# Rearranging the start, the masked KV product and the last tile of a gated SSM and linear-attention kernel under a new instruction order

## The chip, the cores and the metric

The kernel runs on one core of one Trainium2 chip. The metric is device microseconds of one execution. Executions of the same kernel on one core differ by one or two per cent here (163.33 to 166.11 us in 22 executions of the kernel before), so times are medians. An execution counts as slow when it is more than 1.5% above the fastest of its kernel in the same group; the medians below still include slow ones, the ratios do not. The traced execution has a span of its own, about 1.9 us shorter than its time (162.5 us for a time of 164.33 us before); places in the trace are given in microseconds from the start of that span.

## The reference, cut to what matters

The input is x, 2048 positions of 512 features. Two branches are mixed by a gate for each position.

```python
dt = exp(log_dt); Lam_bar = exp(dt * Lam)              # 512 complex poles
for t in range(L):                                      # branch A: a linear recurrence
    h = Lam_bar * h + B_bar @ x[t]
y = 2 * real(hseq @ Cmat.T) + x * Dskip
q, k, v = split(x @ wqkv)                               # branch B: 32 heads of 16
phi_q = concat(softmax(q @ w_phi), softmax(-q @ w_phi)) # 32 features a head
phi_k = concat(softmax(k @ w_phi), softmax(-k @ w_phi))
kv = phi_k.T @ v;  z = sum(phi_k)                       # over all positions
o = (phi_q @ kv) / (phi_q @ z + 1e-6)
g = sigmoid(sum(x * gate_w))
return g * y + (1 - g) * (o @ wo)
```

`kv` needs every position before the first output tile can use it. So there is a seam in the kernel.

## The kernel before

The kernel is a list of tasks, each with an engine, and a tuple `ORDER`, found by a search with assumed costs, that fixes in which order they are emitted; the traces show each engine taking its tasks in that order (VectorE's evacuation of x, whose transposes ended at 4.78 us, started at 6.07, behind the setup copies). Positions are taken in four phases of four tiles of 128.

The setup copies stand ahead of the plan on VectorE:

```python
for h in range(2):
    nc.vector.tensor_copy(out=sel[:, h, h:128:2], in_=ident[0:64, 0:64])
    nc.vector.tensor_copy(out=swap[:, h*64:h*64+64], in_=ident[:, 64-h*64:128-h*64])
# ... mask4, mask16, SM
```

x is transposed on TensorE, evacuated by ScalarE or VectorE, and used by V:

```python
t = pl.add(_pe(4, 128), tr, deps=[d_x[...]], bufs=[b, early[a // 2]])          # 4 transposes
xt[a, f] = evac_task(xT[:, :, tcols(f, a)], b, ..., [t], ("ACT", "DVE"), ...)
# ...
t = pl.add(_pe(4, 512), mm, deps=[xt[a, f], d_wv], bufs=[b])                   # V: 4 matmuls
```

At the seam, the accumulated KV of eight heads is masked to a block diagonal on VectorE, in four instructions, each followed by a small one for the sums `z` (SM). One element is 2 bytes; `(d h)` with h innermost means that the loop below, with d innermost, writes single values 16 bytes apart:

```python
VT(out=KVbd[qr, sgn].rearrange("p g (d h) -> p g h d", d=Dh)[:, :, half*4:half*4+4, :],
   in0=a4[:, :, :, 0:Dh],
   in1=mask4[pr].unsqueeze(1).unsqueeze(3).to_broadcast([64, HG, 4, Dh]), op=ALU.mult)
VT(out=SM[qr, sgn, :, 1, half*4:half*4+4], in0=a4[:, :, :, Dh], in1=..., op=ALU.mult)
```

After it TensorE does small matmuls (`SM`) for the denominators; ScalarE and VectorE make scale factors from them by logarithms and exponentials. For each output tile TensorE makes the numerators (`KVbd`), ScalarE and VectorE scale and add them, a DMA transposes the sum, and TensorE adds its product with Wo to the tile's branch-A matmuls in one PSUM bank. The bank is evacuated with the gate; the last tile's bank in two halves.

Of the kernel before, what the change touches and what calls it, by code (L numbers as in the profile page):

```python
# [18 lines left out]
P = 128  # L19
# [103 lines left out]
def kernel(  # L123
# [47 lines left out]
NWARM = 6  # L171
ORDER = (
    0, 6, 2, 4, 9, 176, 10, 14, 172, 13, 16, 168, 174, 184, 178, 156, 186, 180, 18, 182, 188, 20, 24, 191, 200,
    171, 192, 196, 202, 158, 195, 22, 164, 26, 228, 167, 232, 30, 220, 204, 230, 28, 248, 316, 32, 199, 222, 160,
    34, 132, 788, 36, 206, 78, 134, 234, 244, 138, 163, 236, 318, 154, 38, 794, 49, 792, 250, 136, 224, 240, 208,
    55, 238, 70, 140, 72, 67, 142, 660, 74, 227, 210, 144, 540, 420, 57, 246, 544, 46, 81, 77, 68, 82, 85, 148,
    790, 662, 547, 542, 146, 93, 424, 548, 44, 550, 59, 51, 422, 426, 242, 336, 328, 331, 324, 338, 554, 327, 332,
    796, 150, 42, 664, 334, 152, 667, 556, 558, 372, 346, 340, 376, 350, 514, 553, 96, 798, 53, 40, 668, 374, 348,
    344, 508, 670, 342, 352, 86, 516, 510, 560, 512, 518, 354, 378, 60, 356, 566, 673, 416, 358, 380, 382, 520,
    578, 562, 522, 418, 568, 800, 94, 524, 360, 384, 526, 386, 564, 362, 572, 388, 570, 364, 674, 390, 64, 602,  # L180
    580, 366, 394, 530, 574, 368, 532, 676, 396, 576, 680, 534, 370, 582, 686, 408, 62, 434, 678, 398, 606, 436,
    604, 688, 682, 692, 584, 596, 438, 98, 100, 528, 586, 684, 410, 476, 91, 698, 588, 690, 102, 104, 598, 482,
    108, 694, 400, 402, 700, 428, 106, 600, 590, 446, 696, 486, 702, 404, 112, 480, 448, 608, 484, 478, 610, 612,
    110, 704, 252, 430, 488, 212, 256, 450, 116, 114, 432, 440, 592, 412, 214, 706, 614, 392, 628, 254, 490, 442,
    258, 120, 216, 618, 492, 266, 118, 268, 494, 414, 620, 218, 498, 500, 458, 444, 452, 270, 454, 708, 460, 502,
    622, 88, 710, 504, 260, 124, 122, 616, 506, 536, 496, 538, 634, 406, 456, 712, 262, 630, 722, 278, 462, 716,
    638, 632, 636, 128, 714, 624, 464, 272, 264, 748, 274, 718, 126, 724, 720, 280, 466, 626, 754, 810, 276, 130,
    468, 726, 752, 750, 640, 642, 758, 644, 282, 290, 756, 728, 308, 646, 650, 284, 730, 470, 292, 812, 652, 594,
    732, 760, 734, 816, 762, 814, 648, 764, 286, 654, 738, 804, 320, 294, 820, 288, 808, 740, 472, 766, 656, 296,
    770, 742, 658, 312, 310, 822, 322, 864, 828, 314, 840, 298, 772, 774, 744, 746, 826, 776, 300, 778, 474, 818,  # L190
    834, 866, 782, 824, 786, 806, 868, 832, 784, 780, 870, 846, 842, 302, 882, 880, 876, 844, 836, 830, 878, 838,
    304, 848, 858, 914, 850, 852, 976, 884, 974, 1224, 888, 306, 978, 890, 980, 1230, 862, 892, 854, 894, 916,
    896, 886, 860, 874, 898, 856, 900, 1236, 982, 1072, 872, 908, 984, 1054, 986, 1074, 1056, 1024, 768, 1026,
    1096, 1100, 1102, 910, 988, 1076, 990, 1048, 1078, 920, 1050, 1080, 1218, 1058, 1052, 1030, 1098, 992, 1060,
    1082, 1032, 1226, 1228, 1000, 1062, 1006, 1066, 1222, 922, 994, 996, 1034, 1002, 1028, 1064, 1106, 1036, 1042,
    1234, 1104, 1086, 912, 1084, 902, 1008, 1010, 1232, 1038, 904, 998, 1088, 1238, 1220, 1004, 1108, 1014, 1012,
    918, 906, 1128, 932, 1068, 1040, 1240, 1152, 1110, 1154, 1044, 1146, 1016, 1090, 1070, 1148, 1018, 1200, 1122,
    934, 1248, 1156, 1112, 1130, 1092, 1046, 1132, 1114, 924, 1150, 1246, 1124, 1116, 1118, 1158, 944, 1176, 1244,
    1126, 1242, 1178, 1020, 1094, 1250, 1202, 1194, 1180, 1120, 1184, 1254, 1134, 1170, 1164, 1172, 1022, 1186,
    1160, 926, 1174, 1196, 1136, 1268, 1162, 1208, 936, 1204, 1140, 1252, 1274, 1182, 1256, 1270, 1188, 1138, 938,  # L200
    1346, 1198, 1258, 1166, 1206, 1260, 1340, 928, 940, 736, 1292, 1276, 1278, 942, 1168, 1212, 1298, 1348, 1262,
    1294, 1190, 1142, 1210, 930, 1342, 1214, 802, 1192, 1316, 1272, 1330, 1350, 956, 1344, 1352, 946, 948, 1306,
    1300, 1302, 1280, 1264, 968, 1318, 1322, 1296, 1216, 1266, 1354, 1324, 1356, 1332, 1320, 1326, 1328, 1308,
    950, 1144, 970, 1358, 1286, 1360, 1334, 958, 1304, 952, 1418, 1394, 1362, 1420, 1462, 1388, 1282, 962, 954,
    1396, 1284, 960, 1442, 1310, 1288, 1444, 1412, 1390, 1336, 1446, 1370, 1414, 1416, 1436, 1338, 1450, 1422,
    972, 1290, 1464, 964, 1364, 1372, 1424, 1438, 1366, 1426, 1312, 1378, 1314, 966, 1466, 1374, 1368, 1398, 1430,
    1376, 1392, 1452, 1402, 1428, 1400, 1382, 1432, 1404, 1380, 1440, 1448, 1434, 1406, 1408, 1384, 1454, 1456,
    1411, 1460, 1386, 1458)
# [5 lines left out]
def _pe(n, cols):  # L214
    return {"PE": n * max(30.0, cols / 2.4 + 3.0)}
# [11 lines left out]
def _fast_path(ctx, tc, A_x, A_Lambda_re, A_Lambda_im, A_B_re, A_B_im, A_C_re, A_C_im, A_log_dt, A_Dskip,  # L227
# [101 lines left out]
    nc.gpsimd.iota(iot[:], pattern=[[1, NCH]], base=0, channel_multiplier=0, allow_small_or_imprecise_dtypes=True)  # L329
    nc.gpsimd.memset(dgX[:], 0.0)  # L330
    nc.gpsimd.memset(KVbd[:], 0.0)
    nc.gpsimd.memset(SM[:], 0.0)
    nc.vector.memset(eps_t[:], 1e-6)
    nc.vector.memset(hpi_t[:], float(np.pi / 2.0))
    nc.vector.memset(vx[:, :, :, Dh:Dh + 1], 1.0)
    nc.vector.memset(Zs[:, :, :, 0:ZP], 0.0)
    nc.vector.memset(sel[:], 0.0)
    nc.vector.memset(sg[0:64, :], 1.0)
    nc.vector.memset(sg[64:128, :], -1.0)
    for h in range(2):  # L340
        nc.vector.tensor_copy(out=sel[:, h, h:128:2], in_=ident[0:64, 0:64])
        nc.vector.tensor_copy(out=swap[:, h * 64:h * 64 + 64], in_=ident[:, 64 - h * 64:128 - h * 64])
    nc.vector.tensor_reduce(out=mask4[:], in_=identf[:].rearrange("p (k m) -> p m k", m=4), axis=AX.X, op=ALU.add)
    nc.vector.tensor_reduce(out=mask16[:], in_=identf[:].rearrange("p (g e) -> p g e", e=16), axis=AX.X, op=ALU.add)
    for half in range(2):
        hp = slice(half * 64, half * 64 + 64)
        nc.vector.tensor_copy(out=SM[hp, :, :, 0, half * 4:half * 4 + 4],
                              in_=mask4[hp, :].unsqueeze(1).unsqueeze(1).to_broadcast([64, 2, HG, 4]))

    pl = _Plan({"DVE": 3.8e3, "ACT": 4.2e3, "PE": 1.0e3, "SP": 32.0e3})  # L350
# [40 lines left out]

    bw = pl.buf(*A1)
# [6 lines left out]
    xt = {}  # L399

    def x_block(a):
        pl.unit("x_block")
        for f in range(F):
            b = pl.buf(*A1)

            def tr(e, b=b, f=f):
                for kt in range(KT):
                    nc.tensor.transpose(bfv(b)[:, kt * P:(kt + 1) * P], xn[a][:, f, kt * P:(kt + 1) * P], ident[:])
            t = pl.add(_pe(4, 128), tr, deps=[d_x[a + (a > 0 or f > 1)]], bufs=[b, early[a // 2]])
            xt[a, f] = evac_task(xT[:, :, tcols(f, a)], b, lambda b: bfv(b).rearrange("p (k c) -> p k c", k=KT), [t],  # L410
                                 ("ACT", "DVE"), bf=True, rank=9)

    vt = {}

    def v_unit(ti):
# [7 lines left out]
        t = pl.add(_pe(4, 512), mm, deps=[xt[a, f], d_wv], bufs=[b])  # L423
# [34 lines left out]
    tpv = pl.add({"PE": 200.0}, p_vt, deps=[d_vec], bufs=[bv], rank=10)  # L458
# [26 lines left out]
    tp2 = pl.add({"DVE": 1400.0}, p2, deps=[tp1], rank=10)  # L485
# [35 lines left out]
    tp6 = pl.add({"DVE": 2000.0}, p6, deps=[tp3], rank=4)  # L521
# [10 lines left out]
    tp5 = pl.add({"DVE": 1500.0}, p5, deps=[tp4], rank=-2)  # L532
# [14 lines left out]
    for jj in range(2):  # L547
        parts = []
        for tt in range(4 * jj, 4 * jj + 4):
            parts.append(pl.add({"ACT": 210.0, "DVE": 165.0}, scaled(dgL[:, tt, :], ident[:], lr_[:, ucol(tt)]), deps=[tp3], rank=6 - jj))  # L550
            parts.append(pl.add({"ACT": 210.0, "DVE": 165.0}, scaled(dgS[:, tt, :], swap[:], ns1[:, ucol(tt)]), deps=[tp4], rank=6 - jj))
        t_dl.append(pl.add(_dve(256), lambda e, s_=slice(4 * jj, 4 * jj + 4): VT(out=dgL[:, s_], in0=dgL[:, s_], in1=dgS[:, s_], op=ALU.add),
                           deps=parts, rank=6 - jj))
        for h in range(2):
# [7 lines left out]
            t_dx.append(pl.add({"ACT": 320.0, "DVE": 340.0}, dx, deps=t_dl[-1:], rank=5 - jj))  # L562
    t_dd = [pl.add({"ACT": 210.0, "DVE": 165.0}, scaled(Dd[:, kt, :], ident[:], dsk[:, kt:kt + 1]), deps=[tv], rank=-5) for kt in range(KT)]
# [9 lines left out]
    for j in range(PT):  # L573
        done = []
        for ri in range(2):
            done.append(pl.add(_act(512), lambda e, j=j, ri=ri: nc.scalar.mul(out=tC[:, ri, :], in_=cb.t[:, 1 - ri, j, :], mul=nb2i[:, j:j + 1]),
                               deps=[tp6, t_cl] + tc_b[-2:], bufs=[cb], rank=2))
        for ri, c0 in enumerate((b2r, nb2r)):
# [3 lines left out]
            tc_b.append(pl.add(_dve(512), csc, deps=done, bufs=[cb], rank=2))  # L582
# [1077 lines left out]
```

## Time and profile before

| | before |
|---|---|
| time, median of 3 | 165.34 us (164.89 to 165.54) |
| span of the traced execution | 162.5 us |
| TensorE's wait ahead of V's first matmul, for the x evacuation that stands behind the setup copies | 1.8 us |
| TensorE's wait ahead of the small matmuls, for the KV product | 2.9 us |
| first matmul of the BT group | 23.34 us |
| VectorE's last sum of an output tile ends | 149.86 us |
| TensorE's last matmul to the end of the span | 5.6 us |

The waits come from the list of who waited for whom, the places from the timeline. The views themselves, the busy rows, the stretches, the chain that ended last and the seam, stand in the prediction with their reading.

### The profile page before, as it was taken

The numbers are of one execution on the slowest core, as the hardware profiler recorded it, in microseconds if no ns is written. First come the engines' busy times: TensorE is split into PE (matmuls) and PEld (weight loads), VectorE is DVE, ScalarE is ACT, GpSimd is POOL, SyncE is SP. The second block draws the span as 40 slices with busy tenths as digits, with TensorE's granted clock in tenths as the row PEclk, the third lists the DMA queues.
The fourth block names the chain that finished last, engine by engine and source line by source line (L and its number), as shares of the span: only waits on it lengthen the run. The fifth ranks groups of instructions, "written<-read, shape, count | busy, mean of one in ns | idle before, by whom it ended". The sixth has DMA issues, their size and how long they took to land.

```text
span 162.5 us, 3213 instructions
## 1 busy us (share of the span) xinstructions
PE 149.0 (92%) x1144; PEld 85.4 (53%) x1164; DVE 136.6 (84%) x370; ACT 113.6 (70%) x232; POOL 4.4 (3%) x12
## 2 busy tenths in 40 slices
PE   7599899999999999999999579999999999999960
PEld 2257466655564665655455145755755555554520
DVE  3517999898999899999999997999999999988030
ACT  3158799899878997878989728985892653492120
POOL 8200000000000000000000000000000000000000
PEclk9999999999999999999999969999999999999996
DMA  4989999200000222013522003013323224212531
GB/s 144 343 244 201 164 202 206 61 2 0 0 0 4 65 65 62 5 58 116 121 97 69 0 16 104 13 34 70 99 69 92 68 65 124 70 53 48 115 114 48
DMA packets 29998, 13.93 MB, mean 86 GB/s; under 512 B 23064, under 2 KB 29336, under 8 KB 29976
## 3 DMA queue, kind: packets, MB, share of 16 engines
q1 hardware_dynamic: 29592, 13.59, 34.9%
q8 instruction: 11, 0.18, 0.5%
q10 hardware_dynamic: 384, 0.07, 0.2%
q14 instruction: 11, 0.09, 0.2%
HBM read 3.17 MB, written 2.10 MB: 32 GB/s over the span
## 4 chain that ended last, share of the span: by engine, by line
PE 78%; DVE 9%; ACT 4%; issue 2%; DMA 1%; SPq 1%; ACTq 0%; DVEq 0%
PE pp L982 16%; PE pp L652 12%; PE pp L770 8%; PE pp L860 7%; PE pp L993 7%; PE pp L422 5%; PE pp L967 5%; PE pp L666 4%; DVE KVbd L843 3%; PE pp L801 3%; PE pp L671 2%; PE pp L657 2%; PE pp L927 2%; PE pp L985 2%; DVE xT L381 1%
## 5 line engine op out<-in xcount | busy, mean ns | idle before, releaser
L652 PE MATMUL pp<-xT,BT 128*128 128x512 bf16 x92 | 23.8, 381 | 0.4 <-ACT vx L379 0.2
L982 PE MATMUL pp<-CT,Gs 128*128 128x512 bf16 x93 | 23.2, 379 | 0.2
L970 ACT CAST late<-pp 128x512 bf16<-128x512 f32 x32 | 17.7, 594 | 6.2 <-PE pp L967 5.1
L1003 ACT ACTIVATE late<-pp,Gg 128x512 bf16<-128x512 f32 (+1 forms) x15 | 10.1, 677 | 14.2 <-PE pp L993 5.6
L240 ACT ACTIVATE ET<-pp 128x512 bf16<-128x512 f32 x32 | 17.7, 622 | 2.4 <-PE pp L860 2.3
L422 PE MATMUL pp<-Wv,xT 128*128 128x512 bf16 x62 | 16.8, 397 | 2.5 <-DVE xT L381 1.8
L240 ACT ACTIVATE E<-pp 128x512 bf16<-128x512 f32 x32 | 17.5, 623 | 1.9 <-PE pp L770 1.4
L652 PEld LDWEIGHTS <-BT 128*128 128x128 bf16 x96 | 13.3, 145 | 6.5 <-issue 0.4
L860 PE MATMUL pp<-xT,Wq 128*128 128x512 bf16 x61 | 16.2, 402 | 0.3 <-issue 0.2
L770 PE MATMUL pp<-Wk,xT 128*128 128x512 bf16 x64 | 15.8, 379 | 0.0
L993 PE MATMUL pp<-Wo,late 128*128 128x512 bf16 x60 | 15.4, 379 | 0.2
L974 DVE TENSOR_TENSOR late<-late 128x512 bf16<-128x512 bf16 x32 | 12.6, 416 | 0.8 <-ACT late L970 0.8
L379 ACT CAST Gs<-pp 128x512 bf16<-128x512 f32 x20 | 11.5, 591 | 2.1 <-PE pp L657 1.8
L982 PEld LDWEIGHTS <-Gs 128*128 128x128 bf16 x96 | 8.8, 98 | 7.8
L967 PE MATMUL pp<-KVbd,ET 128*128 128x128 bf16 x128 | 10.9, 219 | 0.1
L422 PEld LDWEIGHTS <-xT 128*128 128x128 bf16 x64 | 6.0, 101 | 8.9 <-DVE xT L381 2.0
L379 ACT CAST vx<-pp 128x512 bf16<-128x512 f32 x16 | 9.0, 591 | 2.3 <-PE pp L422 2.3
L967 PEld LDWEIGHTS <-ET 128*128 128x128 bf16 x128 | 8.6, 98 | 3.6
L860 PEld LDWEIGHTS <-Wq 128*128 128x128 bf16 x64 | 6.3, 103 | 7.3 <-issue 1.7
L794 DVE TENSOR_TENSOR E<-E,rc 128x2048 bf16<-128x2048 bf16 x8 | 9.5, 1217 | 0.2 <-ACT rc L240 0.2
L770 PEld LDWEIGHTS <-xT 128*128 128x128 bf16 x64 | 6.1, 98 | 6.6
L706 DVE TENSOR_TENSOR_SCAN c<-sp,c 128x512 bf16<-128x512 f32 x8 | 9.3, 1207 | 0.0
(172 smaller groups left out, 273.8 us busy)
## 6 DMA issues: line engine op xcount, KB each, us to landing
Zs<-c SPq DMA_DIRECT2D x32, 64.0 KB, 2.1
out_dram<-late SPq DMA_DIRECT2D x15, 128.0 KB, 2.1
xn<-in_A_x_dram SPq DMA_DIRECT2D x3, 512.0 KB, 6.7
CT<-ET SPq DMA_DIRECT2D x8, 128.0 KB, 3.3
xn<-in_A_x_dram SPq DMA_DIRECT2D x2, 256.0 KB, 2.7
Wv<-in_B_wqkv_dram SPq DMA_DIRECT2D x1, 512.0 KB
Wo<-in_B_wo_dram SPq DMA_DIRECT2D x4, 128.0 KB
late<-late SPq DMA_TRANSPOSE x16, 2.4
```

Of the source, the lines that this page charges most:

```text
L240: return nc.scalar.activation(**kw)
L379: nc.scalar.copy(out=o, in_=view(b))
L422: MM(out=f32v(b), lhsT=xT[:, kt, tcols(f, a)], rhs=Wv[:, kt, :], start=(kt == 0), stop=(kt == KT - 1))
L652: MM(out=f32v(b), lhsT=BT[:, kt].rearrange("p r (q t) -> p (r q) t", t=NT)[:, :, j + 4 * h], rhs=xT[:, kt, f * NCH:(f + 1) * NCH], start=( ...
L770: MM(out=f32v(b), lhsT=xT[:, kt, tcols(f, a)], rhs=Wk2[:, kt, :], start=(kt == 0), stop=(kt == KT - 1))
L860: MM(out=f32v(b), lhsT=Wq2[:, kt, g * P:(g + 1) * P], rhs=xT[:, kt, f * NCH:(f + 1) * NCH], start=(kt == 0), stop=(kt == KT - 1))
L967: MM(out=f32v(pn[sgn])[:, g * P:(g + 1) * P], lhsT=ets[f].t[:, sgn, g, cs], rhs=KVbd[:, sgn, g, :], start=True, stop=True)
L970: tn = pl.add(_act(512), lambda e, sgn=sgn: nc.scalar.copy(out=o2.t[:, sgn], in_=f32v(pn[sgn])), deps=[t], bufs=[pn[sgn], o2], rank=rank + 2)
L974: VT(out=v, in0=v, in1=als[f].t[:, a, sgn * H:(sgn + 1) * H].rearrange("p (g h) -> p g h", g=HG).unsqueeze(2).to_broadcast([P, HG, Dh, 8]) ...
L982: MM(out=f32v(py), lhsT=st, rhs=CT[:, tt // 2 + 4 * (tt % 2), :], start=(tt == 0), stop=False)
L993: MM(out=f32v(py), lhsT=oT.t[:, g, :], rhs=Wo[:, g, :], start=False, stop=(g == HG - 1))
L1003: nc.scalar.mul(out=ot.t[:, hs], in_=f32v(py)[:, hs], mul=Gg[:, ti:ti + 1])
```

## The change

The intent: let V start sooner (dependencies of the setup copies as tasks, so that V need not wait for them; two dummy matmuls ahead of it, meant to keep TensorE's clock up), shorten the KV product by writing four values together, evacuate the last tile's halves from two banks side by side, and search the order again with new costs.

```diff
-    for h in range(2):
-        nc.vector.tensor_copy(out=sel[...], ...); nc.vector.tensor_copy(out=swap[...], ...)
+    t_sel = pl.add({"DVE": 280.0}, s_sel, deps=[d_set])      # likewise t_swap, t_mask, t_sm
 ...
+            def dum(e):
+                for _ in range(NDUM):                         # NDUM = 2
+                    MM(out=bd.t[:], lhsT=warm[:, 0:P], rhs=warm[:], start=True, stop=True)
 ...
-                VT(out=KVbd[qr, sgn].rearrange("p g (d h) -> p g h d", d=Dh)[:, :, half * 4:half * 4 + 4, :], in0=a4[:, :, :, 0:Dh],
-                   in1=mask4[pr].unsqueeze(1).unsqueeze(3).to_broadcast([64, HG, 4, Dh]), op=ALU.mult)
+                VT(out=KVbd[qr, sgn].rearrange("p g (d h) -> p g d h", d=Dh)[:, :, :, half * 4:half * 4 + 4],
+                   in0=a4[:, :, :, 0:Dh].rearrange("p g h e -> p g e h"),
+                   in1=mask4[pr].unsqueeze(1).unsqueeze(1).to_broadcast([64, HG, Dh, 4]), op=ALU.mult)
 ...
-            t_kvx.append(pl.add(_dve(256, 16), kx, deps=t_kv[-1:], bufs=[kv[half]], rank=5))
+            t_kvx.append(pl.add({"DVE": 800.0}, kx, deps=t_kv[-1:] + [t_mask], bufs=[kv[half]], rank=5))
 ...
-        py = pl.buf(*A3)
+        pys = [pl.buf(*A3) for _ in range(2 if last else 1)]  # last tile: two banks of 256 columns
 ...
-ORDER = ( 0, 6, 2, 4, 9, 176, ... )
+ORDER = ( 4, 0, 2, 8, 10, 14, ... )                           # found anew
```

Left out are other costs of the search, a fourth output buffer and the split of Wo for the last tile. The new order also moves the 64 small gate matmuls from the start to the seam.

## The prediction

> **What bounds the kernel now.** I read the page first: TensorE's and VectorE's rows of the 40 slices.
> ```profile
> PE   7599899999999999999999579999999999999960
> DVE  3517999898999899999999997999999999988030
> ```
> A slice is 4.06 us. TensorE has two weak places, slices 1 to 5 (4 to 24 us) and 22 to 23 (89 to 98 us), and a tail. VectorE is as full as TensorE from slice 10 to 35. Two engines therefore bound this kernel together: time won on TensorE is kept only if VectorE's queue also ends earlier. Engine busy time by stretch (columns: length, TensorE, weight loads, VectorE, ScalarE, GpSimd, granted clock, DMA share, GB/s) says it in numbers:
> ```profile
> 13.00:25.00 12.00, 11.04 (x120) 6.94 (x120) 11.41 (x47) 10.84 (x24) 0.00 (x0) 1.00 1.14 184
> 65.00:88.00 23.00, 22.79 (x164) 12.31 (x167) 22.93 (x42) 19.84 (x44) 0.00 (x0) 1.00 0.29 81
> 88.00:96.00 8.00, 4.99 (x76) 3.01 (x74) 7.75 (x13) 5.06 (x11) 0.00 (x0) 0.92 0.01 2
> ```
> Between 65 and 88 us both have under 0.25 us idle; in 88 to 96 us TensorE waits and VectorE does not.
>
> Then the chain that ended last (start, duration), at the start:
> ```profile
> 3.60 1.56 DVE sel L341
> 6.07 0.44 DVE xT L381
> 6.55 1.89 PE pp L422 x4
> 8.44 0.85 PE pp L408 x8
> 9.29 0.95 PE pp L422 x4
> 10.46 0.86 PE pp L422 x4
> ```
> A set-up copy of 64x64 takes 1.56 us, so the evacuation of x that releases V starts at 6.07 us, although the first eight transposes ended at 4.78 us. The first four V matmuls then need about 430 ns each (1.72 us), later fours 0.86 us, 216 ns each: TensorE is at half rate until about 9.1 us.
>
> Next the timeline at the KV product:
> ```profile
> 89.01 1.30 DVE L843 TENSOR_TENSOR KVbd<-pp,mask 64x256 bf16<-64x256 f32 x1 [0.17 <-PE pp L801]
> 89.93 0.39 DVE L845 TENSOR_TENSOR SM<-pp,mask 64x16 bf16<-64x16 f32 x1
> 94.42 0.98 PE L927 MATMUL pp<-SM,ET 128*128 128x16 bf16 x32 [2.86 <-DVE SM L845]
> 96.06 2.46 PE L860 MATMUL pp<-xT,Wq 128*128 128x512 bf16 x6 [0.22 <-issue]
> ```
> Four such pairs run from 89.01 to 94.27 us, 1.32 us a pair. TensorE has 12 Q matmuls beside them, then stands 2.86 us, and afterwards runs at half rate (six matmuls in 2.46 us).
>
> Last, the end of the chain:
> ```profile
> 156.31 0.70 ACT late L1003
> 157.01 0.49 DVE late L1005
> 157.53 0.47 ACT late L1003
> ```
> The two half evacuations of the last tile come one after the other.
>
> [...] the granted-clock row does not show the first cold stretch. [...] The old product writes single 2-byte values 16 bytes apart; the new one writes four together, but reads PSUM in 68-byte hops. The old 128x256 product that reads PSUM in runs of eight (L940) takes 415 ns, the KV product 1295; no run yet shows the new pattern. [...]
>
> **The change, part by part.** TensorE's arithmetic is the same but for two dummies (0.86 us at half rate); the last tile has twice the matmuls at half the width. By the instruction order, the first V unit now depends on a ScalarE evacuation, and all four of the first set-up copies still stand ahead of VectorE's x evacuations; what matters is that V no longer waits for them.
>
> Start, TensorE. Transposes end at 4.78; dummies to 5.64; ScalarE's evacuation (4.82 + 0.58 = 5.40) is done by then, so V starts at 5.65 instead of 6.55. If the clock still opens near 9.1 us: 1.72 of V, 0.85 of transposes, then V half cold, 1.3, ends at 9.5 against 10.24. Before the first BT matmul the order then has 48 transposes x 56 ns = 2.7, 36 V matmuls x 216 = 7.8, small ones 0.4: 20.4 us. Before it was 23.34. The lead of 2.9 includes 48 gate matmuls that move to the KV gap (25 ns each, 1.2 us); against that, 0.56 us idle between 23.34 and 32.53 can go. Net 2.3 us.
>
> KV product, TensorE. From 88.98 to 98.15 us it did 20 Q matmuls and 32 small ones, 4.3 + 0.8 = 5.1 us at full rate: 4.1 us lost. In the new order, VectorE does the last rotation (two products of 0.60 and two sums of 0.34, 1.9 us) ahead of the KV product, while TensorE has 16 KV matmuls (0.5), 12 Q matmuls (2.6) and all 64 gate matmuls (1.6). I estimate the new product as midway between 415 ns and its present exclusive 0.92 us, 0.6 with slack, and 0.87 us a pair: 3.5 us. TensorE thus has 4.7 us of work in a 5.4 us wait, about 0.8 idle plus dependencies, say 1.1[...]. Gain 3.0 us.
>
> Tail: side by side instead of in line, 0.5 us. Sum for TensorE: 2.3 + 3.0 + 0.5 = 5.8 us.
>
> VectorE. From its first parameter copy (12.84) to the last sum of a tile (149.86) it is 137.0 us, 5.0 of them idle. The parameter matmuls now follow 20 transposes instead of three V units, so they end near 11 us: 1.6 earlier. KV pairs: 4 x (1.32 - 0.87) = 1.8 less. Engine choices: x copies 9 to 6 (-1.0), Gs copies 4 to 2 (-1.2), c copies 0 to 2 (+1.2), diagonals 9 to 12 (+0.5), a final evacuation (+0.65), mask copies now inside the stretch (+0.25): +0.4. Better order: perhaps 1.0 of the idle. Sum 1.6 + 1.8 - 0.4 + 1.0 = 4.0, with the tail 4.5.
>
> The smaller sum binds: 4.5 us. I take off 0.4 for new waits that a searched order always meets, and get 4.1: 165.34 - 4.1 = 161.2 us.
>
> **Rivals.** (a) ScalarE takes over at the start. It gets three more x evacuations (10 against 7) and stays strictly in line with a 1.28 us table load at 13 to 15 us; the PSUM slots of V then come free late. For it: in 13 to 25 us ScalarE was already busy 10.84 of 12, and the chain before ran through it until 24.5. Against: the order puts one table function and several diagonals later. It would eat 1 to 1.5 us of TensorE's lead: 161.5 to 162.5.
> (b) VectorE is the bound and the early lead is hidden: only the KV saving and the tail remain, 165.34 - 1.8 - 0.5 = 163.0. For it: VectorE's 99.7% in 65 to 88 us. Against: its own chain also starts earlier.
> (c) The PSUM hops make the new product as slow as the old: VectorE loses 1.8 of its gain and TensorE's gap grows by 1.8, about 163.
> (d) The dummies open the clock[...]: V saves another 1.7 us, but x lands until about 10 us (last loads 6.7 us after issue at 3.6) and the evacuations follow; maybe 0.5 more, 160.7.
> (e) Loads gate the BT matmuls: issued at 11.2 with 6.8 us to landing, 18.0, ahead of 20.4; no effect.
>
> **Range and chances.** With (a) and part of (b) together the gain is 2.3, 163.0; with (d) and a denser order 5.8, 159.5. 2% faster lies at 162.03, 0.8 us above my value. Faster by over 2%: 0.70; within: 0.29; slower: 0.01.
>
> **What would show it.** V's first matmul near 5.65 us; the first BT matmul at 20.4 to 21.5; KV pairs near 0.87 us; TensorE's wait at the small matmuls under 1.2 us and no half-rate Q matmuls after it; VectorE's last tile sum near 145.5; the last half evacuations side by side. I am wrong if VectorE's last sum has moved by less than 3 us, if KV pairs stay above 1.1 us, or if idle time comes up in 10 to 35 us on TensorE because of ScalarE.

## The result

The changed kernel took 161.23 us, the median of four executions (161.54, 159.85, 163.4 and 160.92, of which 163.4 counts as slow), against 165.23 us for the kernel before (164.89 to 165.54). Ratios in this text are the mean time of one kernel's fast executions over that of the other's of the same rounds, so they are not quite the ratio of the quoted medians. The ratio is 0.973, with a 95% interval of 0.966 to 0.980: faster. The value predicted was 161.2 us. That the sum came out says little about its terms, as the profile shows.

The busy rows of the changed kernel's page, in 40 slices of 3.99 us:

```profile
PE   7769999999999999999999999997899999999950
...
DVE  3427998999999999999999998989979999977050
```

TensorE's hole at the seam is gone, and there is a new one in slices 27 and 28 (108 to 116 us). VectorE, which had a 9 in every slice from 25 to 34 before, now has an 8 in slices 26 and 29. The same in numbers, by stretch (columns as in the prediction):

```profile
13.00:25.00 12.00, 12.00 (x72) 6.65 (x70) 11.26 (x59) 11.30 (x25) 0.00 (x0) 1.00 1.00 185
65.00:88.00 23.00, 23.00 (x153) 11.80 (x152) 22.86 (x42) 20.83 (x48) 0.00 (x0) 1.00 0.21 61
88.00:96.00 8.00, 8.00 (x161) 5.63 (x158) 7.68 (x25) 7.97 (x17) 0.00 (x0) 1.00 0.18 57
106.00:125.00 19.00, 17.14 (x154) 9.93 (x151) 18.02 (x52) 11.03 (x24) 0.00 (x0) 1.00 0.42 74
```

In 88 to 96 us TensorE is busy for all 8.00 us, where it had 4.99, and the granted clock is 1.00 and not 0.92. In 106 to 125 us it stands 1.86 us; before it stood 0.12.

The timeline of the changed kernel at the start (start, duration, engine, line, output and inputs, number; in brackets the idle time before and what ended it):

```profile
4.57 1.06 PE L438 MATMUL pp<-warm 128*128 128x512 bf16 x2
...
5.64 1.02 PE L451 MATMUL pp<-Wv,xT 128*128 128x512 bf16 x4
...
8.14 0.40 PE L426 MATMUL pp<-ident,xn 128*128 128x128 bf16 x4 [1.25 <-DMA xn<-in_A_x_dram]
...
11.97 0.17 PE L482 MATMUL pp<-ident,vec_n 20*128 20x20 bf16 x1 [1.26 <-DMA vec_n<-in_gate_w_dram]
```

V's first matmul starts at 5.64 us, as predicted, and its four take 1.02 us against 1.89: the clock is open. But TensorE then waits 1.25 us for x and 1.26 us for the parameter vectors. The first BT matmul starts at 21.74 us, against 23.34 before and 20.4 predicted; and 1.2 us of what it gained is the gate matmuls (48 of 25 ns in the trace before), which only moved.

The seam, from the same timeline (L872 and L875 are the product, L957 the small matmuls, L1031 Wo):

```profile
90.41 0.42 DVE L872 TENSOR_TENSOR KVbd<-pp,mask 64x256 bf16<-64x256 f32 x1
...
90.75 0.16 DVE L875 TENSOR_TENSOR SM<-pp,mask 64x16 bf16<-64x16 f32 x1
...
94.04 0.95 PE L957 MATMUL pp<-SM,ET 128*128 128x16 bf16 x32
...
112.44 1.04 PE L1031 MATMUL pp<-Wo,late 128*128 128x512 bf16 x4 [1.86 <-DMA late<-late]
```

The four pairs run from 90.41 to 92.50 us, so 0.52 us a pair, where they took 1.32. There is no wait before L957, but it starts 1.5 us after the product is done, because the order has put Q and gate matmuls there. And at 112.44 us a Wo group has waited 1.86 us for a transposing DMA.

The end, from the same timeline; SPq is SyncE's DMA queue:

```profile
144.72 0.49 ACT L1036 ACTIVATE late<-pp,Gg 128x256 bf16<-128x256 f32 x1
...
152.59 3.68 SPq L1039 DMA_DIRECT2D out_dram<-late  x4
...
153.59 0.69 ACT L1036 ACTIVATE late<-pp,Gg 128x512 bf16<-128x512 f32 x1 [7.19 <-PE pp L1031]
153.97 0.48 DVE L1038 TENSOR_SCALAR late<-pp,Gg 128x256 bf16<-128x256 f32 x1 [0.36 <-PE pp L1031]
```

Only the second half of the last tile is evacuated at the end (the 128x256 of VectorE). The first was evacuated at 144.72 us, so the two do not stand side by side, which the prediction had expected. The last half evacuation ends at 154.45 us, 0.51 us after TensorE's last matmul at 153.94; before, these two were 158.00 and 156.91, so 1.09 us apart. Yet TensorE's last matmul to the end of the span is 5.7 us, where it was 5.6. VectorE's last tile sum ended at 147.39 us, 2.5 us earlier than before, less than the 3 us below which the prediction called itself wrong.

So three questions: which part gains what; what the start is bound by; and where the new waits behind the seam come from.

### The profile page after: what moved, and what is told of

It reads as the page before. It is cut to its first block, busy times and chain, and to the rows that moved or that the text cites.

```text
span 159.6 us, 3263 instructions
## 1 busy us (share of the span) xinstructions
PE 148.3 (93%) x1178; PEld 85.9 (54%) x1178; DVE 133.8 (84%) x371; ACT 113.9 (71%) x231; POOL 4.4 (3%) x12
## 4 chain that ended last, share of the span: by engine, by line
PE 84%; DMA 9%; DVE 1%; ACT 1%; SPq 1%; issue 0%
PE pp L1015 15%; PE pp L681 13%; PE pp L890 9%; PE pp L799 9%; PE pp L1031 8%; PE pp L451 8%; PE pp L695 4%; PE pp L999 4%; DMA xn<-in_A_x_dram 4%; DMA late<-late 3%; PE pp L830 3%; DMA vec_n<-in_gate_w_dram 2%; PE pp L700 2%; PE pp L686 2%; PE pp L1019 2%; PE pp L957 1%
## 5 line engine op out<-in xcount | busy, mean ns | idle before, releaser
L1015 PE MATMUL pp<-CT,Gs 128*128 128x512 bf16 (+1 forms) x104 | 23.7, 363 | 0.0
L1036 ACT ACTIVATE late<-pp,Gg 128x512 bf16<-128x512 f32 (+1 forms) x14 | 9.5, 675 | 15.4 <-PE pp L1031 13.1
L241 ACT ACTIVATE ET<-pp 128x512 bf16<-128x512 f32 x32 | 17.0, 618 | 1.3 <-PE pp L890 1.2
L1031 PE MATMUL pp<-Wo,late 128*128 128x512 bf16 (+1 forms) x68 | 16.1, 367 | 1.9 <-DMA late<-late 1.9
L890 PE MATMUL pp<-xT,Wq 128*128 128x512 bf16 x64 | 15.6, 378 | 0.0
L451 PE MATMUL pp<-Wv,xT 128*128 128x512 bf16 x64 | 15.3, 379 | 0.0
L371 ACT CAST Gs<-pp 128x512 bf16<-128x512 f32 x22 | 13.0, 594 | 1.7 <-PE pp L686 1.4
L1015 PEld LDWEIGHTS <-Gs 128*128 128x128 bf16 x104 | 9.5, 98 | 7.5
L1031 PEld LDWEIGHTS <-late 128*128 128x128 bf16 x68 | 6.0, 98 | 6.6 <-DMA late<-late 2.0
```

The lines of the kernel that those rows point to most:

```text
L241: return nc.scalar.activation(**kw)
L371: nc.scalar.copy(out=o, in_=view(b))
L451: MM(out=f32v(b), lhsT=xT[:, kt, tcols(f, a)], rhs=Wv[:, kt, :], start=(kt == 0), stop=(kt == KT - 1))
L890: MM(out=f32v(b), lhsT=Wq2[:, kt, g * P:(g + 1) * P], rhs=xT[:, kt, f * NCH:(f + 1) * NCH], start=(kt == 0), stop=(kt == KT - 1))
L1015: MM(out=f32v(py)[:, 0:w], lhsT=st, rhs=CT[:, tt // 2 + 4 * (tt % 2), n * w:n * w + w], start=(tt == 0), stop=False)
L1031: MM(out=f32v(py)[:, 0:w], lhsT=oT.t[:, g, :], rhs=Wo[:, g, hs], start=False, stop=(g == HG - 1))
```

## The experiments

All kernels here gave correct results. Those from e0 to e3 ran together, then e4 to e7, then e8 to e11; each group had its own executions of the kernel before beside it. The table has what the experiments turn on; "first BT" and "last PE" are the start of the first BT matmul and the end of TensorE's last matmul in the traced execution.

| run | median us | ratio to before (95%) | first BT | last PE |
|---|---|---|---|---|
| before (e0's group) | 164.95 | 1 | 23.34 | 156.91 |
| e0, the change again | 161.97 | 0.984 (0.976 to 0.992) | 21.93 | 154.05 |
| e1, the change with the old KV product | 163.95 | 0.994 (0.990 to 0.997) | slow | slow |
| e2, before with the new KV product | 160.52 | 0.975 (0.969 to 0.980) | 22.90 | 152.24 |
| e3, the change without dummies | 161.84 | 0.982 (0.976 to 0.988) | 22.19 | 153.39 |
| e4, the change, last output by ScalarE's queue | 161.21 | 0.977 (0.973 to 0.981) | 21.47 | 153.14 |
| e5, the change, vectors early | 161.03 | 0.975 (0.970 to 0.980) | 20.78 | 153.26 |
| e6, e2 with setup copies behind | 159.86 | 0.970 (0.966 to 0.974) | 22.56 | 151.91 |
| e7, e2 with vectors early | 160.60 | 0.970 (0.964 to 0.975) | 23.51 | 152.87 |
| e8, the change, small matmuls first | 161.83 | 0.985 (0.980 to 0.989) | 21.74 | 153.86 |
| e9, e8 with vectors early | 160.62 | 0.976 (0.971 to 0.981) | 21.05 | 153.19 |
| e10, e6 with vectors early | 160.31 | 0.972 (0.968 to 0.977) | 22.98 | 152.32 |
| e11, e2 in runs of 4 bytes | 160.30 (one) | | 23.33 | 152.97 |

(The places of "before" are those of its trace above. e1's traced execution fell in the slow state, so its places are not compared.)

### e0: the changed kernel again

No edit.

> The changed kernel once more, unaltered, as the yardstick for the runs beside it. Its four executions on record scatter from 159.85 to 163.4 us while those of the kernel before lie within 0.65 us, and its profile has one wait of 1.9 us of TensorE for a transposing DMA near 112 us, in a slice where the DMA engines are 80% busy at only 70 GB/s. Theory chance: that wait is an accident of one execution; this profile lacks it or has it elsewhere, and its span is then 1 to 2 us shorter. Rival order: the new order of instructions makes the wait; it stands at the same place with 1.5 us or more. Either way the ratio to the kernel before is 0.966 to 0.980.

Measured: 161.97 us, ratio 0.984, which is outside the interval expected for it by 0.004. The ten executions of the change seen so far have a median of 161.7 us; the first result was on the lucky side. The list of TensorE's waits, with the total, the number and the longest:

```profile
PE pp L1031 <- DMA late<-late: 1.0, 1, 1.0
PE pp L999 <- DVE qmax L967: 0.7, 1, 0.7
```

The wait for the transposing DMA is there again, at 112.45 us, 1.0 us and not 1.9. It is in every trace of the new order, with 0.6 to 1.9 us in all, and in none of the old order. So the place belongs to the new kernel, most likely to its order, as the rival said (no run changes the order alone), and its length is partly chance. Why the DMA is late I could not settle: in the first trace its issue began at 107.49 us, a second one began 1.3 us later, and the wait ended at 112.43; in e0 these were 108.34, 1.3 us later and 112.44. The page gives 2.4 us from issue to landing as the median.

### e1: the change with the old KV product

```diff
-   [:, :, :, half*4:half*4+4], in0=a4.rearrange("p g h e -> p g e h"), in1=mask4 over (g, d)
+   [:, :, half*4:half*4+4, :], in0=a4, in1=mask4 over (g, ..., d)        # as before
```

> The changed kernel with only the masked KV product put back to its old loop (2-byte writes 16 bytes apart); order and all else as changed. Theory A: the product is what closes TensorE's hole, so a pair goes back from 0.53 us to about 1.3, VectorE needs 3.2 us more between the last KV product of TensorE and the small matmuls, TensorE stands 2.5 to 3.2 us and may run slow for some us after it: 3.0 to 4.5 us over the changed kernel (163.5 to 165.5 us). Rival B, the prediction's own sum: the KV part is worth no more than about 1.8 us because VectorE's sum binds: 162.5 to 163.3 us.

Measured: 163.95 us, ratio 0.994; 7 of its 18 executions were slow. The median lies in theory A's range, but only 2.0 us over e0's. By the ratios of fast runs the new product is worth 0.9935 - 0.9838 = 0.0097 of 164.95, or 1.6 us, within the changed kernel: about half of the least that A said, and what B said. But B's reason does not hold, as e2 shows: the new order simply covers a slow product better. In the trace:

```profile
92.47 1.31 DVE L872 TENSOR_TENSOR KVbd<-pp,mask 64x256 bf16<-64x256 f32 x1
...
93.41 0.39 DVE L874 TENSOR_TENSOR SM<-pp,mask 64x16 bf16<-64x16 f32 x1
...
97.84 0.85 PE L956 MATMUL pp<-SM,ET 128*128 128x16 bf16 x28 [1.07 <-DVE SM L874]
```

The product is as slow as before, but TensorE waits 1.3 us in all for it (0.26 and 1.07) and not 2.9, since Q and gate matmuls fill the rest. (The traced execution was slow: these durations are compared, not its time.) The other finding is that everything else in the change together, new order, start and tail, gains 0.65% (0.3 to 1.0), or about 1.1 us.

### e2: the kernel before with the new KV product alone

The edit is the KV product's three lines of the change, on the kernel before.

> The kernel before with only the masked KV product changed to runs of 8 bytes; its old order and everything else stay. Theory A: the KV product alone holds most of the gain, pairs go from 1.32 to about 0.55 us, TensorE's 5.4 us wait falls to about 2.3 with no stretch at a lower clock: 161.0 to 162.2 us, a gain of 3 to 4.2 us, as much as the whole change. Rival B: only VectorE's own 1.8 us: 163.2 to 163.8 us. Rival C: the old order has VectorE work waiting behind, which fills the time won: under 1 us.

Measured: 160.52 us (159.66 to 160.80), ratio 0.975: 4.2 us faster than before, and faster than the whole change in the same rounds. Theory A said 161.0 at best. The product, and the stretches 88 to 96, 96 to 106 and 106 to 125 us:

```profile
88.56 0.42 DVE L843 TENSOR_TENSOR KVbd<-pp,mask 64x256 bf16<-64x256 f32 x1 [0.17 <-PE pp L801]
88.91 0.16 DVE L846 TENSOR_TENSOR SM<-pp,mask 64x16 bf16<-64x16 f32 x1
...
88.00:96.00 8.00, 8.00 (x109) 4.70 (x106) 7.72 (x25) 7.48 (x16) 0.00 (x0) 1.00 0.10 33
96.00:106.00 10.00, 9.86 (x104) 6.14 (x103) 9.93 (x32) 9.50 (x23) 0.00 (x0) 1.00 0.22 55
106.00:125.00 19.00, 19.00 (x175) 11.37 (x173) 18.93 (x56) 12.41 (x27) 0.00 (x0) 1.00 0.32 78
```

In the old order TensorE has no hole at the seam either once the product is short, and none behind it: 0.14 us idle in 37 us, where the changed kernel's first trace has 1.90. VectorE saved 4 x 0.8 = 3.2 us itself. The gain is larger, by the traces because the half-rate stretch behind the hole went too (before, six Q matmuls took 2.46 us from 96.06 us and the granted clock was 0.92 in 88 to 96 us and 0.90 in 96 to 106; in e2 it is 1.00 in both). (Of this trace's lead, 0.4 us lies at the start, where V's first group happened to run at full rate, in 1.04 us and not 1.89. e11, below, starts as the kernel before did, and its last matmul still ends 3.9 us earlier.) The mean granted clock of all 22 executions of before lies at 0.972 to 0.990, of the six of e2 at 0.990 to 0.994.

Together, each as one less its ratio, times 164.95 us: the new product alone 4.2 us, all the rest alone about 1.1 us, both 2.7 us, in the same rounds. The two parts do not add, because both close the same hole; and beside the new product, the rest costs some 1.5 us. The intervals of e0 and e2 overlap; but in these same rounds every execution of e2 (up to 160.80 us) is below every one of e0 (from 161.27). The size of the loss is loose: e3 and e8, which leave the change as fast as it was, give 0.982 and 0.985, yet its first result gave 0.973 and e4 0.977. The mean of these five ratios, 0.980, against e2's 0.975 makes it about 0.9 us (other rounds, so an estimate). Every version of the old order with the new product gives 0.970 to 0.975.

### e3: no dummies

```diff
-NDUM = 2
+NDUM = 0
```

> The changed kernel without the two dummy matmuls ahead of V; order unchanged. Theory A: the start is set by when x and the parameter vectors land, so the dummies move nothing that counts: within 0.4 us of the changed kernel; the first V tile starts 1.1 us sooner or as soon as its evacuation ends (near 5.0 us), and it may run at half rate (1.7 us) or not. Rival B: the dummies hold the clock open; without them V0 and V1 and the transposes after them run at half rate and the parameters come later: 0.9 us or more slower.

Measured: 161.84 us, 0.1 us from e0: theory A. The timeline:

```profile
5.93 1.86 PE L451 MATMUL pp<-Wv,xT 128*128 128x512 bf16 x4 [1.16 <-DMA Wv<-in_B_wqkv_dram]
...
8.45 1.91 PE L451 MATMUL pp<-Wv,xT 128*128 128x512 bf16 x4
```

Both V groups run at half rate in this trace and take 0.85 us longer each than in e0. But the time saved there goes into waits for DMAs: the first BT matmul starts at 22.19 us against 21.93. Over all profiles, the first V group ran at full rate in 6 of 7 with dummies (1.02 to 1.13 us) and in 1 of 7 without (1.04 us in e2; the other six 1.85 to 1.89). That this is the dummies' doing is not shown. In e0 the clock was open before they began, as it was in e1, e5 and e8:

```profile
3.72 0.68 PE L426 MATMUL pp<-ident,xn 128*128 128x128 bf16 x8
4.24 0.59 PE L438 MATMUL pp<-warm 128*128 128x512 bf16 x2
```

The eight transposes ahead of the dummies take 0.68 us here (0.70, 0.82 and 0.86 in e1, e5 and e8) and 1.06 in e3, where nothing ahead of them differs; the two dummies take 0.59 us in these four. Only in the first trace of the change and in e9 did the clock open after the dummies had begun (dummies 1.06 us in both, V's first group 1.02 and 1.13); in e4 dummies (1.06 us) and V's first group (1.77 us) both stayed near half rate.

### e4: the last output by ScalarE's queue

```diff
-(nc.scalar if last and e == "ACT" else nc.sync).dma_start(...)
+(nc.scalar if last else nc.sync).dma_start(...)
```

> The changed kernel with one word changed: the last half tile's output DMA is issued by ScalarE's queue and not by SyncE's. In the changed kernel's profile the last evacuation ended at 154.45 us, but its DMA was issued at 154.81 and took 1.46 us to issue on SyncE behind three others, so the time from TensorE's last matmul to the end of the span stayed at 5.7 us as before, although the split saved 0.6 us of evacuation. Theory A: that issue sits on the end path; 0.8 to 1.4 us faster than the changed kernel (about 160.6 to 161.2 us), TensorE's end to span's end near 4.5 us. Rival B: the end waits for the data of the four outputs to land whoever issues them: under 0.3 us.

Measured: 161.21 us. That looks like theory A, but the trace says B:

```profile
153.18 0.48 DVE L1038 TENSOR_SCALAR late<-pp,Gg 128x256 bf16<-128x256 f32 x1 [0.36 <-PE pp L1031]
153.70 0.34 ACTq L1039 DMA_DIRECT2D out_dram<-late  x1
```

The last issue now follows the evacuation at once and takes 0.34 us and not 1.46. The span still ends at 158.8 us, 5.1 us after the last evacuation, as in the changed kernel (154.45 to 159.6), and 5.7 us after TensorE's last matmul. What this execution gained it had earlier: TensorE's last matmul ended at 153.14 us, against 153.94 and 154.05.

The landings recorded in the traces say what the end waits for. In all eight traces of the new order the span ends 1.84 us after the last output has landed. In the seven with SyncE's issue (1.46 to 1.88 us long) it ends 3.2 to 3.4 us after that issue, so there the issue does lie on the end path. In e4 the issue ends at 154.04 us, but the output comes in 16 parts, and one of them lands at 156.96, the others by 155.92. So taking the issue away bared a late part behind it and won 0.4 us at most: from the last evacuation to the end it is 5.1 us here and 5.2 to 5.5 in the seven. In the old order this is 4.5 us before, and 4.5, 4.3 and 4.9 us in e2, e6 and e7; the last output lands 2.4 to 2.6 us after the last evacuation there, and 3.3 to 3.7 in the new order. That ate the tail's gain. Why one part lands late stays open.

### e5: the parameter vectors early

```diff
+    nc.sync.dma_start(out=xn[1], in_=x4[1])
+    for n, src in enumerate(vsrc):
+        nc.sync.dma_start(out=vec_n[4*n:4*n+4, :], ...)      # from behind x and Wc
-    for a in range(1, 4):
+    for a in range(2, 4):
         nc.sync.dma_start(out=xn[a], in_=x4[a])
```

> The changed kernel with the five parameter loads issued on SyncE's queue after the second x block and not after the fourth. Their landing holds TensorE for 1.2 to 1.3 us near 12 us in both profiles of the changed kernel and the chain of parameters behind it. Theory A: that wait is the start's bound; it falls under 0.3 us, the first BT matmul moves from 21.9 to about 21.0 us, 0.5 to 1.0 us faster than the changed kernel. Rival B: five issues (2 us of SyncE's queue) ahead of the last two x blocks delay these by as much, the wait moves to the transposes of x: no gain, or a loss up to 0.5 us.

Measured: 161.03 us, ratio 0.975 against e0's 0.984: theory A by size, though the intervals overlap. Against e4 (161.21 us), which ran in the same rounds and starts as the change does, it is only 0.2 us, so the size is not shown here; e9 against e8, below, gives 1.2 us. The wait for the vectors is gone. Part of it comes back:

```profile
9.77 1.29 PE L427 MATMUL pp<-ident,xn 128*128 128x128 bf16 x20 [0.98 <-DMA xn<-in_A_x_dram]
```

TensorE's waits for x are 1.9 us, where they were 1.3 us in the first trace of the change and 1.6 in e0. The first BT matmul starts at 20.78 us, 1.0 us earlier than in the first trace of the change. So by these waits loads, more than the order of instructions, bound this start.

### e6 and e7: parts of the start in the old order

e6 is e2 with the setup copies in a function that VectorE calls after its first evacuation of x:

```diff
                 nc.vector.tensor_copy(out=o, in_=view(b))
+                if held:
+                    held.pop()()          # sel, swap, masks
```

e7 is e2 with the edit of e5.

> The kernel before with the new KV product and, besides, its setup copies moved behind VectorE's first evacuation of x; the old order otherwise. It tells what the setup part is worth by itself. Theory A: V's first matmul moves from 6.55 to 5.5 to 6.0 us, where Wv's DMA lands, and the transposes after it wait for x and the vectors as long as before: within 0.4 us of the KV product alone (160.1 to 160.6 us). Rival B, the prediction: the whole 0.9 us of V's start carries to the end: 159.5 to 159.8 us.

> The kernel before with the new KV product and the five parameter loads issued after the second x block. Theory A: as in the run with early vectors on the changed kernel, the 0.9 us wait of TensorE near 12 us goes: 159.6 to 160.1 us, the fastest so far. Rival B: x comes later by as much: 160.3 to 161.0 us.

Measured: e6 159.86 us, e7 160.60 us, both with the ratio 0.970. e6 lies between its two theories: V's first matmul moved to 5.24 us, where it waited for Wv's DMA, the vectors were still waited for (1.0 us), and the first BT matmul moved by 0.34 us. e7 met rival B by its median: the wait for the vectors is gone, but V's first two groups ran at half and partly at half rate (1.89 and 1.33 us) in its trace, and the first BT matmul came 0.6 us later than in e2. The intervals of e2, e6 and e7 overlap.

### e8: the small matmuls first

The order's entries of one Q group, the last 16 gate matmuls and that group's exponentials go behind the first small matmuls:

```diff
-... 1232, 844, 1242, 794, 800, 892, 882, ... 888, 846, 890, 978, 105, 886, 848, ...
+... 1232, 1242, 794, 892, 882, ... 888, 890, 978, 105, 886, 844, 800, 846, 848, ...
```

> The changed kernel with one edit of its order: one group of Q matmuls, the last 16 gate matmuls and the two exponentials of that Q group move from ahead of the first small matmuls to behind them. In both profiles of the changed kernel the KV product is done near 92.6 us, but TensorE starts the small matmuls only at 94.0 to 94.2, since the order puts a filler there that was sized for a product of 0.8 us a pair while it takes 0.53. Theory A: those 1.5 us delay the chain from the small matmuls to the scale factors and the output tiles, which shows later as TensorE's waits of 0.7 us for qmax and 1.0 to 1.9 us for the transposing DMA; small matmuls start near 92.8, these waits shrink below 0.6 us together, 0.8 to 1.7 us faster than the changed kernel: 160.0 to 161.0 us. Rival B: VectorE is full there and decides when output tiles are ready: the waits stay and the time is within 0.4 us of 161.5.

Measured: 161.83 us: no gain, rival B by size. My theory fell. The trace shows how:

```profile
92.77 0.95 PE L956 MATMUL pp<-SM,ET 128*128 128x16 bf16 x32
...
94.64 1.57 ACT L240 ACTIVATE ET<-pp 128x512 bf16<-128x512 f32 x3 [0.75 <-PE pp L889]
...
96.08 0.41 ACT L240 ACTIVATE q<-pp 128x256 f32<-128x256 f32 x1
...
101.55 0.73 PE L998 MATMUL pp<-KVbd,ET 128*128 128x128 bf16 x8 [1.02 <-DVE qmax L966]
```

The small matmuls do start 1.4 us sooner than in e0 (94.22). But the next step of the chain, the logarithm on ScalarE (`q<-pp`), starts at 96.08 us and not at 95.47 as in e0: in ScalarE's line it stands behind exponentials of Q. It now even stood idle before them for 0.75 us, as their matmuls had moved back. Everything after it comes at the same time, and the wait for qmax is 1.02 us. In e2 this logarithm starts at 92.12 us, and the first scale factors are made at 96.11 us against 99.89 in e0 and 100.01 here. In e0, too, ScalarE is busy with these exponentials until 95.47 us, so moving TensorE's work alone cannot bring the scale factors forward: the order on ScalarE holds them as well. That is read from the traces; no run put the exponentials behind the logarithm.

### e9 and e10: combinations

e9 is e8 with the early vectors; e10 is e6 with them.

> The same edit of the order together with the parameter loads behind the second x block, on the changed kernel. Theory A: the two gains add, as one lies before 22 us and the other after 92 us on TensorE's path: 159.0 to 160.2 us. Rival B: as for either part alone, 160.4 to 161.3 us.

> The kernel before with the new KV product, the setup copies behind the first evacuation of x, and the parameter loads behind the second x block; old order, no dummies. Alone, the copies brought 159.86 and the loads 160.6 us. Theory A: with V ahead and no wait for the vectors the start is about 0.7 us shorter than with the copies alone: 158.9 to 159.6 us, the fastest of all. Rival B: V's first tiles run at half rate as in both runs before, and x comes later: 159.7 to 160.5 us.

Measured: e9 160.62 us, rival B, 1.2 us below e8 in the same rounds, so the gain of the vectors alone; e10 160.31 us, rival B, not better than e6: V's first two groups took 1.87 and 1.70 us, at half rate, so the earlier vectors were not waited for, and V was late instead. The best version is e6, with 159.86 us and a ratio of 0.970 (0.966 to 0.974), below the whole interval of the change in e0, though not below that of its first result (0.966 to 0.980). Against e2 it is not separated.

### e11: runs of 4 bytes

```diff
-   one VT of [64, HG, Dh, 4]
+   for hp in range(2):  # two VT of [64, HG, Dh, 2], each writing two values together
```

> The kernel before with each masked KV product as two instructions of 128 elements a partition, written in runs of 4 bytes, in place of one of 256 in runs of 8. Counted from start to start, the old one takes 0.94 us (256 pieces written), the new one 0.34 (64 pieces). Theory A: pieces cost, not elements: each half instruction writes 64 pieces too and takes 0.30 to 0.36 us, 0.65 a pair of halves, so with the sums a pair of products is 0.85 to 0.9 us. Rival B: elements cost and the pieces only above some size: 0.18 to 0.22 us each, and the pair stays at 0.55 to 0.6. It says too whether the prediction's 0.87 us for a pair was the cost of 4-byte runs. Result correct; time 161.0 to 162.5 us by theory A.

Measured, one look: 160.3 us, correct. The timeline (the two halves are merged):

```profile
89.00 0.48 DVE L845 TENSOR_TENSOR KVbd<-pp,mask 64x128 bf16<-64x128 f32 x2 [0.17 <-PE pp L801]
89.41 0.16 DVE L848 TENSOR_TENSOR SM<-pp,mask 64x16 bf16<-64x16 f32 x1
```

From the start of the first to the start of SM, the two halves take 0.41 us, 0.2 each: rival B. In e2 the one instruction takes 0.35 (88.56 to 88.91). My estimate from the two: 0.06 us fixed and 1.1 ns an element, for runs of 4 and of 8 bytes alike. The old loop's 0.92 us (89.01 to 89.93) is then 3.4 ns an element. The step lies between one and two values written side by side, not at the number of places written to. Two other differences can be set aside. The old loop reads PSUM in order and the fast ones in hops, so that reading is not what makes it slow. And it repeats each mask value 16 times in a row; but so does the product BD (L621 before), which writes side by side and takes 0.20 us from start to start for 128 elements (21.82 to 22.02), the fast rate.

## Why the prediction was right or wrong

**Start, TensorE, "net 2.3 us": wrong.** "V starts at 5.65" was right (5.64 us), and the clock opened sooner, as rival (d) had it (V's first four matmuls in 1.02 us and not 1.89), though not clearly through the dummies (e3). The step that failed is "before the first BT matmul the order then has 48 transposes ... 20.4 us": it counted TensorE's work and left out when x and the vectors land. TensorE waited 2.5 us for them. The first BT matmul came 1.6 us earlier, 1.2 of it being moved gate matmuls: net about 0.4. In e3, 1.7 us of faster V made no difference that shows (0.1 us), while earlier vectors were worth 1.2 us in e9 against e8; in the old order they brought nothing that shows (e10 against e6). Rival (e) looked at loads, but at those of BT only, and was right on these.

**KV product, TensorE, "gain 3.0 us": right in kind, too small.** The mis-sized term is the pair: "midway between 415 ns and its present exclusive 0.92 us" gave 0.87 us, and it took 0.52. Alone in the old order the product is worth 4.2 us (e2); within the change only 1.6 (e1), as the new order hides part of a slow product. The 0.87 us was the estimate, with no run of the new pattern behind it; by e11 two values written together are as fast per element as four (0.41 us for two instructions of 128 elements, against 0.35 us for one of 256 in e2, which leaves 0.06 us for the second instruction). Rival (c), that the hops in PSUM make it slow, is refuted by 0.42 us.

**Tail, "0.5 us": wrong.** The step that failed is "side by side": the first half was evacuated nine microseconds before the second (144.72 and 153.97 us), so no run shows halves from two banks side by side. The second did end 0.6 us sooner after the last matmul, but its output landed 3.3 us after that and not 2.4, and TensorE's end to the end of the span stayed at 5.7 us. e4 shows that SyncE's long issue is not all of it.

**VectorE, "the parameter matmuls ... end near 11 us: 1.6 earlier": wrong.** The first parameter copy started at 12.44 us against 12.84, 0.4 earlier, again because the vectors had not landed.

**"The smaller sum binds: 4.5 us": wrong.** VectorE's last tile sum moved 2.5 us in the change, and in e2 it moved 4.7 us (149.86 to 145.18), though only 3.2 us of VectorE's work had gone. By the traces it followed what it is fed by.

**"I take off 0.4 for new waits": the term that made the sum come out.** The new waits of TensorE after 96 us are 1.9 us in the first trace of the change and 1.7 in e0. Rival (a) named ScalarE, but for the start, where TensorE was busy 12.00 of 12 us between 13 and 25; by the traces it is at the seam that ScalarE's line delays the chain.

So the total was right because a start and a tail that gained little, and a remainder (by the traces its order) that costs 0.9 to 1.5 us, were set off by a product worth more than expected. It was luck, and in part that of the first four executions: by e0's ratio the gain is 2.7 us, not the 4.1 forecast. Why the change's executions scatter more than those of before is not settled. DMA landings and the clock's state at the start differ between its traces (first BT at 21.93, 21.47 and 21.74 us in e0, e4 and e8, which share the start), which is a candidate only.

## What to carry to other kernels

Run the smallest part of a bundle by itself: here three lines in the old order beat the whole change in the same rounds. An order found by a search is fitted to its cost table, and this one reckoned 0.8 us for a product that takes 0.52, so its filler stood in front of the small matmuls (though moving that alone, in e8, gained nothing); measure first, then search. And before paying for an engine's early start, list when each load lands.

## Costs measured here, and what stays open

- VectorE's writes of single 2-byte values, 16 bytes apart, took about 3.4 ns an element, against 1.1 ns for two or four values together (estimates from 0.92, 0.41 and 0.35 us).
- The unchanged small instruction behind such a product (SM, 64x16) took 0.39 us after the slow one and 0.16 after the fast one. Each time it ends within 0.1 us of the product, so it may only have waited for the product's end.
- These runs give no odds for a short burst of dummies: the first real group ran at full rate (1.02 to 1.13 us) in 6 of 7 profiles with two dummies and in 1 of 7 without (1.04 us), but in 4 of the 6 the clock was open before the dummies began (eight transposes in 0.68 to 0.86 us, against 1.06).
- A transposing DMA within SBUF landed later than usual in some places: 2.4 us from issue in the median, but nearly 5 us for the one issued at 107.49 us in the first trace of the change and 4.1 us at 108.34 in e0, both taken to the end of TensorE's wait (112.43 and 112.44 us). The cause is open.
